# Narrowing weights on dense buffers, w_out's forms in w_in's ring, both score halves in one PSUM bank

## The chip, the cores and the metric

The kernel runs on one core of a Trainium2 chip. The metric is the device time of one execution in microseconds (us); the time shown is the median of the runs. The profile comes from one execution, and its times are counted from the first instruction of the program.

The engines are called by short names. PE is TensorE, which multiplies matrices, and PEld is its loading of weights, which overlaps the multiplying. DVE is VectorE, ACT is ScalarE, POOL is GpSimd, and SP is SyncE, which here does nothing but issue DMAs. L12 is line 12 of the kernel before.

## What is computed

Channel attention on q, k, v (4 batches, 6080 tokens, 256 channels), then a feed-forward layer with Gelu:

```python
qn = q / (norm(q, axis=1) + 1e-06);  kn = k / (norm(k, axis=1) + 1e-06)
s = kn.transpose(0, 2, 1) @ qn / tau          # 256 x 256 for each batch
a = softmax(s, axis=-1)                       # denominator + 1e-09
x = (v @ a).reshape(24320, 256)
h = x @ w_in                                  # 256 -> 2048
out = gelu(h) @ w_out                         # 2048 -> 256
```

q, k and v are float32. w_in and w_out reach the kernel as 64-bit floats, two 32-bit words to a value, and are narrowed on the chip.

## The kernel before

**Arithmetic.** A float32 operand is split into a high part in the matmul's own type (fp32r) and a low part that holds the rest. A product is then three matmuls: high by low, high by high, low by high. The softmax's matrix is multiplied into w_in for each batch (`w_group`, `w_product`), so v goes straight into the feed-forward layer. Most products of blocks are made by a scheme with seven products in place of eight. It needs sums of blocks, the forms: `v_sums` for v, `w_adds` for w_in, `wo_adds` for w_out. `wo_forms`, `wo_adds`, `wo_hi` and `wo_lo` (L586 to L615) make the forms S1 to S4 of w_out from its plain blocks, four times, once for each group g, and store them to DRAM (`keep_out`), from where all later steps load them again.

**Prelude.** The scores of batch 0 are plain float32 matmuls (`qk_first`, L431) while q and k stream in. `qk_fill` begins batch 1's scores: 16 float32 matmuls, each of them two instructions in the profile (L443), which are put between the stages of the first softmax. `GAPS` says how many go before the stages' matmuls, and what is left over runs after `w_group(0, 0)`.

**Narrowing.** There are 16 units of weights, 512 values a partition each: two units for each of four groups of w_in and eight for w_out. `load_unit` loads one as pairs of 32-bit words into a ring `raw` of three buffers (or, for two of them, into `raw_w`), and `narrow_unit` calls `narrow` (L520 to L549). Of a pair, word 1 is `high` and word 0 is `low`; both are views with a step of two words. `narrow` clamps `high`, squares it on ACT, shifts and merges its bits, masks by the square, scales `low` by the exponent, and leaves high and low parts of the float32 value. Of its ten steps, eight are on DVE (L532, L537, L539, L541, L544, L545, L548, L549) and two on ACT (L534, L547). Clamped and merged values are written back into `high`, in the strided buffer. Scratch is `nt` in the prelude, and then by turns the buffers `kqc` and `osb` of the main part. Narrowed units are stored to DRAM too (`keep`, L1107); stores that come early are held and issued after the loads of q and k.

Five units are narrowed in the prelude and eleven in the part that follows, `paces` of them after each step u. Units 0 to 3 are w_in's groups 0 and 1; unit 4 is the first of w_out, and `pair_out` multiplies by it during u = 1.

**Plain part.** Eight steps u make the first 1024 tokens with ordinary block products (`plain_products`, L847 to L849). `pair_out` (L981 to L983) multiplies Gelu's blocks of the step before by w_out, interleaved with them.

**Main part.** After that come steps of one chunk and one group each, with seven products (`chunk_ops`, L903 to L905), Gelu (L930, L933), the splitting of its result (L936, L954) and the products with w_out (`chunk_out`). Four more kinds of work are hung on these steps by number: the sums of v, the forms of w_out (step g + 1 of the first four), the next batch's scores, and its softmax with its w_groups.

**Next batch's scores.** `burst(b, k, m)` multiplies four splits of k and q for one half m of the channels: for each, one matmul of 512 columns (high k by high and low q) and one of 256 (low k by high q). It writes to the bank that this step has spare. `burst_sum` adds the bank to `sacc` in SBUF, once for each half. There are 34 pairs of bursts. Softmax adds `sacc`'s two halves (high and low) at its start (L636).

**What sets the order.** The prelude keeps the order in which it is written and its priorities. From `w_group(0, 0)` on, a planner (`Order`) takes all instructions of PE, ACT, DVE and SP, keeps PE's order as written, gives each other instruction a latest start from PE's nominal times, and runs a list schedule with modelled durations 24 times, each time earlier for what PE waited on; the best order is fixed for each engine. Buffers in rings (`RINGS`: raw 3, hl 2, wo 4, win 2) must be taken in turn. The model's durations count elements and know nothing of steps between them. Each engine runs its own order strictly, so an instruction that waits holds up all behind it; SP's DMAs are one such queue.

Of the kernel before, what the change touches and what calls it, by code (L numbers as in the profile page):

```python
# [9 lines left out]
F32 = mybir.dt.float32  # L10
# [307 lines left out]
GAPS = (7, 4, 2)  # L318
# [17 lines left out]
def channel_attention_gelu_ffn(ctx, tc, qk, kqt, vt, tau, w_in, w_out, out):  # L336
# [100 lines left out]
    def qk_fill():  # L437
# [9 lines left out]
        acc = state["sacc"] = pm.tile([P, NCT, NT], F32, name="sacc")  # L447
        nc.gpsimd.memset(acc[:, :, C:], 0.0)
        for m in range(NCT):
            nc.vector.tensor_copy(out=acc[:, m, 0:C].rearrange("p (b a) -> p b a", a=2), in_=paired(s[:, m]))  # L450
# [19 lines left out]
    def burst(b, k, m):  # L470
        cs = slice(m * P, (m + 1) * P)
        s = state["burst"] = spare()
        ops = [(hls[b, k * NB + t], j) for t in range(NB) for j in range(JS)]
        for i, (hl, j) in enumerate(ops):
            nc.tensor.matmul(s, hl[:, 0, j, 0, cs], hl[:, :, j, 1].rearrange("p h (a b) -> p h b a", a=2), start=(i == 0), stop=False,
                             skip_group_check=True)
            nc.tensor.matmul(s[:, 0:C], hl[:, 1, j, 0, cs], paired(hl[:, 0, j, 1]), start=False,
                             stop=(i == len(ops) - 1), skip_group_check=True)

    def burst_sum(k, m):  # L480
        s = state.pop("burst")
        if k == 0:
            if m == 0:
                state["sacc"] = pm.tile([P, NCT, NT], F32, name="sacc")
            nc.vector.tensor_copy(out=state["sacc"][:, m], in_=s)
        else:
            acc = state["sacc"][:, m]
# [21 lines left out]
    def load_w(src):  # L509

        if len(units) in (11, 12):
# [6 lines left out]
    def narrow(hi, lo, raw):  # L518
# [4 lines left out]

        if "filled" not in state:
            tmp = pst.tile([P, 2, n], F32, name="nt", bufs=2)
        else:
            state["nt"] = not state.get("nt")
            tmp = pg.tile([P, 2, n], F32, name="kqc" if state["nt"] else "osb", bufs=1)

        top = high.bitcast(F32)  # L530
# [12 lines left out]
        body = high  # L543
# [42 lines left out]
    def wo_forms(g):  # L586
        whole = pg.tile([P, 8 * H], F32, name="osb")
        x = whole.rearrange("p (s f q n) -> p s f q n", s=2, f=4, q=2)
        hl = whole[:, 0:4 * H].rearrange("p (f h q n) -> p f h q n", f=2, h=2, q=2).bitcast(F32R)
        return x, [pg.tile([P, 2, 2, 2, P], F32R, name="kqc", bufs=1), hl]  # L590
# [15 lines left out]
    def wo_hi(x, hl):  # L606
        for i in range(2):
            nc.scalar.copy(out=hl[i][:, :, 0], in_=x[:, 1, 2 * i:2 * i + 2])

    def wo_lo(g, x, hl):  # L610
        for i in range(2):
            nc.vector.tensor_tensor(out=hl[i][:, :, 1], in0=x[:, 1, 2 * i:2 * i + 2], in1=f32(hl[i][:, :, 0]),
                                    op=ALU.subtract)
# [878 lines left out]
```

## Time and profile before

| | |
|---|---|
| median of 3 runs | 2061.69 us (2061.46 to 2065.83) |
| the profiled execution | 2062.65 us, span of its instructions 2060.9 us |
| granted PE clock, mean | 0.997 |
| busy: PE, PEld, DVE, ACT | 99%, 95%, 90%, 79% of the span |
| chain of work that ended last | PE 87%, DVE 6%, DMA 3%, ACT 2%, issue 1% |

A row of a group gives line, engine and operation, then output and inputs by the program's names, the shapes, how often, the busy time and the mean duration. A row of the waits gives the engine and line that waited, what ended the wait, the total in us, how often, and the longest. A row of a timeline gives start, duration and instruction, and in brackets how long the engine was idle before it and what ended that. A row of a stretch gives its ends, its length, busy time and instruction count of PE, PEld, DVE, ACT and POOL, the granted PE clock (1.00 is full), the DMA engines' share and GB/s. Matmuls are pipelined: a busy time of a single one is longer than the distance to the next, which is what counts.

### The profile page before, as it was taken

The numbers are of one execution on the slowest core, as the hardware profiler recorded it, in microseconds if no ns is written. First come the engines' busy times: TensorE is split into PE (matmuls) and PEld (weight loads), VectorE is DVE, ScalarE is ACT, GpSimd is POOL, SyncE is SP. The second block draws the span as 40 slices with busy tenths as digits, with TensorE's granted clock in tenths as the row PEclk, the third lists the DMA queues.
The fourth block names the chain that finished last, engine by engine and source line by source line (L and its number), as shares of the span: only waits on it lengthen the run. The fifth ranks groups of instructions, "written<-read, shape, count | busy, mean of one in ns | idle before, by whom it ended". The sixth has DMA issues, their size and how long they took to land.

```text
span 2060.9 us, 40753 instructions
## 1 busy us (share of the span) xinstructions
PE 2032.2 (99%) x15958; PEld 1962.3 (95%) x15958; DVE 1857.9 (90%) x2733; ACT 1620.7 (79%) x2720; POOL 1.3 (0%) x8
## 2 busy tenths in 40 slices
PE   8899999999999999999999999999999999999999
PEld 7778999999999999999999999999999999999999
DVE  6899899899899989999989999999998998898897
ACT  6666788888888888888988877777787777777776
POOL 0000000000000000000000000000000000000000
PEclk9999999999999999999999999999999999999999
DMA  9556687877787778687678666666556566566664
GB/s 376 177 187 220 225 277 239 270 262 258 245 298 253 244 252 273 223 279 257 225 267 267 206 225 225 215 211 213 198 185 224 177 200 214 189 202 206 199 196 166
DMA packets 153808, 475.31 MB, mean 231 GB/s; under 512 B 16016, under 2 KB 26256, under 8 KB 153104
## 3 DMA queue, kind: packets, MB, share of 16 engines
q1 hardware_dynamic: 153616, 472.71, 68.3%
q8 instruction: 125, 2.05, 0.4%
q14 instruction: 67, 0.55, 0.1%
HBM read 435.16 MB, written 37.49 MB: 229 GB/s over the span
## 4 chain that ended last, share of the span: by engine, by line
PE 87%; DVE 6%; DMA 3%; ACT 2%; issue 1%; SPq 0%; DVEq 0%; ACTq 0%
PE po L1038 10%; PE po L1037 10%; PE po L1036 10%; PE pb L903 5%; PE pb L904 5%; PE pb L905 5%; PE pa L903 5%; PE pa L904 5%; PE pa L905 5%; PE po L1020 4%; PE po L1022 4%; PE po L1021 4%; DMA raw<-qk 2%; PE pz L904 2%; PE pz L905 2%; PE pz L903 2%
## 5 line engine op out<-in xcount | busy, mean ns | idle before, releaser
L1038 PE MATMUL po<-los,wo 128*128 128x256 f32 (+1 forms) x1890 | 520.3, 275 | 0.8 <-DVE los L954 0.8
L1036 PE MATMUL po<-his,wo 128*128 128x256 f32 (+1 forms) x1890 | 520.4, 275 | 0.0
L1037 PE MATMUL po<-his,wo 128*128 128x256 f32 (+1 forms) x1890 | 519.9, 275 | 0.0
L936 DVE TENSOR_TENSOR los<-gs,his 128x512 fp32r<-128x512 f32 (+1 forms) x601 | 407.0, 682 | 67.9 <-ACT gs L930 53.4
L1036 PEld LDWEIGHTS po<-his,wo 128*128 128x128 f32 x1890 | 362.7, 192 | 1.9
L1038 PEld LDWEIGHTS po<-los,wo 128*128 128x128 f32 x1890 | 362.9, 192 | 1.3 <-DVE los L954 1.2
L1037 PEld LDWEIGHTS po<-his,wo 128*128 128x128 f32 x1890 | 362.9, 192 | 0.5
L954 DVE TENSOR_TENSOR los<-gs,his 128x1024 fp32r<-128x1024 f32 (+1 forms) x270 | 326.6, 1210 | 18.2 <-ACT his L950 16.6
L950 ACT CAST his<-gs 128x1024 fp32r<-128x1024 f32 (+1 forms) x270 | 281.2, 1043 | 75.3 <-DVE gs L947 73.2
L903 PE MATMUL pa<-vhi,wl 128*128 128x256 f32 (+1 forms) x920 | 253.3, 275 | 4.7 <-DVE pz L917 4.4
L903 PE MATMUL pb<-vhi,wl 128*128 128x256 f32 (+1 forms) x920 | 253.6, 276 | 3.1 <-ACT gs L930 1.3
L904 PE MATMUL pa<-vhi,wh 128*128 128x256 f32 (+1 forms) x920 | 253.2, 275 | 0.0
L905 PE MATMUL pa<-vlo,wh 128*128 128x256 f32 (+1 forms) x920 | 253.2, 275 | 0.0
L905 PE MATMUL pb<-vlo,wh 128*128 128x256 f32 (+1 forms) x920 | 253.1, 275 | 0.0
L904 PE MATMUL pb<-vhi,wh 128*128 128x256 f32 (+1 forms) x920 | 253.1, 275 | 0.0
L943 DVE TENSOR_TENSOR gs<-gs 128x1024 f32<-128x1024 f32 (+1 forms) x135 | 163.7, 1213 | 29.8 <-ACT gs L930 26.2
L903 PEld LDWEIGHTS pa<-vhi,wl 128*128 128x128 f32 x920 | 176.2, 191 | 9.9 <-DVE pz L917 5.8
L903 PEld LDWEIGHTS pb<-vhi,wl 128*128 128x128 f32 x920 | 176.3, 192 | 6.9 <-ACT his L933 1.5
L933 ACT ACTIVATE his<-px 128x512 fp32r<-128x512 f32 (+1 forms) x184 | 108.8, 591 | 90.7 <-PE px L905 88.6
L904 PEld LDWEIGHTS pa<-vhi,wh 128*128 128x128 f32 x920 | 176.3, 192 | 3.6
L904 PEld LDWEIGHTS pb<-vhi,wh 128*128 128x128 f32 x920 | 176.3, 192 | 2.4
L905 PEld LDWEIGHTS pa<-vlo,wh 128*128 128x128 f32 x920 | 176.8, 192 | 0.0
(284 smaller groups left out, 5138.7 us busy)
## 6 DMA issues: line engine op xcount, KB each, us to landing
wo<-keep_out SPq DMA_DIRECT2D x503, 512.0 KB, 4.5
raw<-qk SPq DMA_DIRECT2D x95, 512.0 KB, 6.1
kqc<-kqt SPq DMA_DIRECT2D x72, 512.0 KB, 5.1
wo<-keep_out SPq DMA_DIRECT2D x135, 256.0 KB, 4.0
v_raw<-vt SPq DMA_DIRECT2D x40, 512.0 KB, 6.6
out<-osb SPq DMA_DIRECT2D x40, 512.0 KB, 5.1
win<-keep_in SPq DMA_DIRECT2D x24, 512.0 KB, 6.1
keep_in<-win SPq DMA_DIRECT2D x4, 1024.0 KB, 4.4
```

Of the source, the lines that this page charges most:

```text
L903: nc.tensor.matmul(o, wls[g][:, a, q], paired(vh[:, at, :h]), start=start, stop=False, skip_group_check=True)
L904: nc.tensor.matmul(o, whs[g][:, a, q], paired(vh[:, at, :h]), start=False, stop=False, skip_group_check=True)
L905: nc.tensor.matmul(o, whs[g][:, a, q], paired(vl[:, at, :h]), start=False, stop=stop, skip_group_check=True)
L933: nc.scalar.activation(out=slot(name)[0], in_=t[SOURCE[name]], func=AF.Gelu)
L936: tt(out=slot(name)[1], in0=whole(name), in1=f32(slot(name)[0]), op=ALU.subtract)
L943: tt(out=g4[:, 0:2], in0=g4[:, 1:3], in1=g4[:, 0:2], op=ALU.subtract)
L950: nc.scalar.copy(out=views[1][:, 2 - 2 * i:4 - 2 * i], in_=views[0][:, 2 * i:2 * i + 2])
L954: tt(out=views[2][:, at], in0=views[0][:, 2 * i:2 * i + 2], in1=f32(views[1][:, at]), op=ALU.subtract)
L1020: nc.tensor.matmul(o, w[:, 1, q], mh, start=start, stop=False, skip_group_check=True)
L1036: nc.tensor.matmul(o, w[:, 1, q], mh, start=starts and q == 0, stop=False, skip_group_check=True)
L1037: nc.tensor.matmul(o, w[:, 0, q], mh, start=False, stop=False, skip_group_check=True)
L1038: nc.tensor.matmul(o, w[:, 0, q], ml, start=False, stop=stops and q == 1, skip_group_check=True)
```

## The change

1. *Narrowing.* Once the main buffers are open, `narrow` puts the clamped value, the merged bits and the mask into a dense buffer (`p5`, or a third part of `osb`), in place of word 1 of the raw pairs.
2. *w_out's first unit.* The prelude narrows four units in place of five; the fifth, and the stores that were held, come after `w_group(0, 0)`, in the planned part. Its raw words go to the ring `raw`.
3. *Fills.* `GAPS` is 10, 4, 2, so that all 16 float32 matmuls of batch 1 stand among the stages of the first softmax and none after `w_group(0, 0)`.
4. *Forms of w_out.* Their high and low parts lie in one buffer of the ring `win` in place of `kqc` and half of `osb`; one cast and one subtraction of 1024 values replace two of 512. The two stores stay.
5. *Scores.* The two halves m share one PSUM bank, 256 columns each. The matmul of 512 columns becomes two of 256, all three products are added up in PSUM, one addition to `sacc` replaces two, `sacc` has half the size, and softmax takes its values from there without adding halves.

```diff
@@ -315,7 +315,7 @@
 
 NARROWS = (4, 9)
 
-GAPS = (7, 4, 2)
+GAPS = (10, 4, 2)
 
 TOP_MAX = (2.0 - 2.0 ** -3 - 2.0 ** -23) * 2.0 ** 16
 TOP_MIN = 1.125 * 2.0 ** -15
@@ -444,10 +444,9 @@
                     s[:, m], raw[:, j, 0, m * P:(m + 1) * P], raw[:, j, 1], start=(i == 0 and m == 0),
                     stop=(i == FILL * JS - 1), skip_group_check=True)
                 yield
-        acc = state["sacc"] = pm.tile([P, NCT, NT], F32, name="sacc")
-        nc.gpsimd.memset(acc[:, :, C:], 0.0)
+        acc = state["sacc"] = pm.tile([P, NCT, C], F32, name="sacc")
         for m in range(NCT):
-            nc.vector.tensor_copy(out=acc[:, m, 0:C].rearrange("p (b a) -> p b a", a=2), in_=paired(s[:, m]))
+            nc.vector.tensor_copy(out=acc[:, m].rearrange("p (b a) -> p b a", a=2), in_=paired(s[:, m]))
 
 
     def sum_up(nps, acc, start, stop):
@@ -469,22 +468,21 @@
 
     def burst(b, k, m):
         cs = slice(m * P, (m + 1) * P)
-        s = state["burst"] = spare()
-        ops = [(hls[b, k * NB + t], j) for t in range(NB) for j in range(JS)]
-        for i, (hl, j) in enumerate(ops):
-            nc.tensor.matmul(s, hl[:, 0, j, 0, cs], hl[:, :, j, 1].rearrange("p h (a b) -> p h b a", a=2), start=(i == 0), stop=False,
-                             skip_group_check=True)
-            nc.tensor.matmul(s[:, 0:C], hl[:, 1, j, 0, cs], paired(hl[:, 0, j, 1]), start=False,
+        if m == 0:
+            state["burst"] = spare().rearrange("p (m c) -> p m c", m=NCT)
+        s = state["burst"][:, m]
+        ops = [(hls[b, k * NB + t], j, x) for t in range(NB) for j in range(JS) for x in ((1, 0), (0, 0), (0, 1))]
+        for i, (hl, j, (x, y)) in enumerate(ops):
+            nc.tensor.matmul(s, hl[:, x, j, 0, cs], paired(hl[:, y, j, 1]), start=(i == 0 and m == 0),
                              stop=(i == len(ops) - 1), skip_group_check=True)
 
-    def burst_sum(k, m):
+    def burst_sum(k):
         s = state.pop("burst")
         if k == 0:
-            if m == 0:
-                state["sacc"] = pm.tile([P, NCT, NT], F32, name="sacc")
-            nc.vector.tensor_copy(out=state["sacc"][:, m], in_=s)
+            state["sacc"] = pm.tile([P, NCT, C], F32, name="sacc")
+            nc.vector.tensor_copy(out=state["sacc"], in_=s)
         else:
-            acc = state["sacc"][:, m]
+            acc = state["sacc"]
             nc.vector.tensor_tensor(out=acc, in0=s, in1=acc, op=ALU.add)
 
     norms = {}
@@ -508,7 +506,7 @@
 
     def load_w(src):
 
-        if len(units) in (11, 12):
+        if len(units) == 12:
             raw = pst.tile([P, src.shape[-1], 2], U32, name="raw_w", bufs=2)
         else:
             raw = pqk.tile([P, src.shape[-1], 2], U32, name="raw", bufs=3)
@@ -521,13 +519,18 @@
         n = raw.shape[1]
         low, high = raw[:, :, 0], raw[:, :, 1]
 
+        own = None
         if "filled" not in state:
             tmp = pst.tile([P, 2, n], F32, name="nt", bufs=2)
         else:
             state["nt"] = not state.get("nt")
-            tmp = pg.tile([P, 2, n], F32, name="kqc" if state["nt"] else "osb", bufs=1)
-
-        top = high.bitcast(F32)
+            if state["nt"]:
+                tmp, own = pg.tile([P, 2, n], F32, name="kqc", bufs=1), pg.tile([P, NT], F32, name="p5")
+            else:
+                tmp = pg.tile([P, 3, n], F32, name="osb", bufs=1)
+                own = tmp[:, 2]
+
+        top = high.bitcast(F32) if own is None else own
         body, w, tail = tmp[:, 0].bitcast(U32), tmp[:, 0], tmp[:, 1]
         nc.vector.tensor_scalar(out=top, in0=high.bitcast(F32), scalar1=TOP_MAX, scalar2=-TOP_MAX,
                                 op0=ALU.min, op1=ALU.max)
@@ -540,7 +543,7 @@
                                        op0=ALU.bitwise_and, op1=ALU.bitwise_or)
         nc.vector.scalar_tensor_tensor(out=w, in0=tail, scalar=TOP_MIN ** 2, in1=top, op0=ALU.is_ge, op1=ALU.mult)
 
-        body = high
+        body = topu
         nc.vector.tensor_scalar(out=body, in0=w.bitcast(U32), scalar1=0xFF800000, scalar2=None, op0=ALU.bitwise_and)
         nc.vector.scalar_tensor_tensor(out=tail, in0=low, scalar=2.0 ** -52, in1=body.bitcast(F32), op0=ALU.mult,
                                        op1=ALU.mult)
@@ -586,8 +589,8 @@
     def wo_forms(g):
         whole = pg.tile([P, 8 * H], F32, name="osb")
         x = whole.rearrange("p (s f q n) -> p s f q n", s=2, f=4, q=2)
-        hl = whole[:, 0:4 * H].rearrange("p (f h q n) -> p f h q n", f=2, h=2, q=2).bitcast(F32R)
-        return x, [pg.tile([P, 2, 2, 2, P], F32R, name="kqc", bufs=1), hl]
+        t = pw.tile([P, 2, NCT, NT], F32R, name="win", bufs=2)
+        return x, t.rearrange("p a b n -> p (a b n)").rearrange("p (f h q n) -> p f h q n", f=4, h=2, q=2)
 
     def wo_adds(g, x):
         fa, fs = x[:, 0], x[:, 1]
@@ -604,15 +607,12 @@
         tt(out=s4, in0=a12, in1=s2, op=ALU.subtract)
 
     def wo_hi(x, hl):
-        for i in range(2):
-            nc.scalar.copy(out=hl[i][:, :, 0], in_=x[:, 1, 2 * i:2 * i + 2])
+        nc.scalar.copy(out=hl[:, :, 0], in_=x[:, 1])
 
     def wo_lo(g, x, hl):
-        for i in range(2):
-            nc.vector.tensor_tensor(out=hl[i][:, :, 1], in0=x[:, 1, 2 * i:2 * i + 2], in1=f32(hl[i][:, :, 0]),
-                                    op=ALU.subtract)
-        nc.sync.dma_start(out=keep_out[g][:, 0:4:3], in_=f32(hl[0]))
-        nc.sync.dma_start(out=keep_out[g][:, 4:6], in_=f32(hl[1]))
+        nc.vector.tensor_tensor(out=hl[:, :, 1], in0=x[:, 1], in1=f32(hl[:, :, 0]), op=ALU.subtract)
+        nc.sync.dma_start(out=keep_out[g][:, 0:4:3], in_=f32(hl[:, 0:2]))
+        nc.sync.dma_start(out=keep_out[g][:, 4:6], in_=f32(hl[:, 2:4]))
 
 
     def preload(func, after):
@@ -627,14 +627,11 @@
         rk, nms, dens = (small[:, 16 + 2 * i:18 + 2 * i] for i in range(3))
         ts = []
         for m in range(NCT):
-            t = pm.tile([P, C], F32, name=f"t{m}")
             if first:
+                t = pm.tile([P, C], F32, name=f"t{m}")
                 nc.scalar.copy(out=t, in_=state["s"][m])
             else:
-                s = state["sacc"]
-                both = s[:, m].rearrange("p (h b a) -> p h a b", h=2, a=2)
-                nc.vector.tensor_tensor(out=t.rearrange("p (a b) -> p a b", a=2), in0=both[:, 0], in1=both[:, 1],
-                                        op=ALU.add)
+                t = state["sacc"][:, m]
             ts.append(t)
         nsum = state.pop("nsum")
         if first:
@@ -669,8 +666,12 @@
         if not first:
             yield
         for m in range(NCT):
-            nc.vector.scalar_tensor_tensor(out=ts[m], in0=ts[m], scalar=rk[:, m:m + 1], in1=rq[:, 0:C],
-                                           op0=ALU.mult, op1=ALU.mult)
+            t, x, o = ts[m], rq[:, 0:C], ts[m]
+            if not first:
+                o = ts[m] = pm.tile([P, C], F32, name=f"t{m}")
+                t = t.rearrange("p (b a) -> p a b", a=2)
+                x, o = (y.rearrange("p (a b) -> p a b", a=2) for y in (x, o))
+            nc.vector.scalar_tensor_tensor(out=o, in0=t, scalar=rk[:, m:m + 1], in1=x, op0=ALU.mult, op1=ALU.mult)
             nc.vector.reduce_max(out=nms[:, m:m + 1], in_=ts[m], axis=AX.X, negate=True)
         yield
         es = []
@@ -1154,10 +1155,8 @@
             narrow_unit()
         if 14 <= js < 18:
             v_split_first((B11, B21, B12, B22)[js - 14])
-    for _ in range(3):
+    for _ in range(2):
         narrow_unit()
-    for x in held:
-        keep(*x)
     fill = qk_fill()
     stages = softmax(True, ps_o, "po2")
     with tc.high_priority():
@@ -1186,6 +1185,9 @@
     body = nc.cur_bb.bb.instructions
     opened = len(body)
     w_group(0, 0)
+    narrow_unit()
+    for x in held:
+        keep(*x)
     for _ in fill:
         pass
     for _ in range(3):
@@ -1243,7 +1245,8 @@
             w = (4 if b == 1 else 3) + 3 * k
             for m in range(NCT):
                 put(n0 + w, "PE", burst, b, k, m)
-                put(n0 + w, "PEdve", burst_sum, k, m)
+            put(n0 + w, "PEdve", lambda: None)
+            put(n0 + w, "PEdve", burst_sum, k)
             for i in range(NB):
                 js = k * NB + i
                 put(max(0, n0 + w - 4 + i), "load", load_qk, b, js)
```

## The prediction

> **What bounds the kernel now.** I read the busy times by stretch first, to find where TensorE (PE) is not full.
>
> ```profile
> 80.00:160.00 80.00, 76.92 (x344) 65.46 (x343) 79.06 (x133) 53.59 (x92) 0.00 (x0) 0.98 0.56 175
> ...
> 240.00:500.00 260.00, 260.00 (x2136) 254.48 (x2136) 237.36 (x329) 219.39 (x369) 0.00 (x0) 1.00 0.78 264
> 500.00:530.00 30.00, 28.28 (x221) 26.73 (x220) 26.81 (x54) 29.24 (x50) 0.00 (x0) 1.00 0.66 222
> ```
>
> The columns are PE, weight loads, VectorE (DVE), ScalarE (ACT), GpSimd, clock, DMA share, GB/s. From 240 us on PE has no gap (260.00 of 260), so there every extra matmul costs its full time, and work taken from DVE buys nothing. From 80 to 160 us it is DVE that is full (79.06 of 80) and PE that has holes. So the change can win only ahead of 240 us and can lose behind it. Who waits for whom between 60 and 240 us:
>
> ```profile
> PE pa L847 <- DVE wl L721: 4.2, 1, 4.2
> ...
> DVE raw L532 <- DMA raw<-w_out: 3.6, 1, 3.6
> PE pa L903 <- DVE pz L917: 3.4, 2, 3.0
> ...
> DVE osb L598 <- DMA keep_out<-osb: 1.3, 1, 1.3
> ```
>
> Each PE hole has a tail, which the clock column of narrower stretches shows:
>
> ```profile
> 69.58:75.21 5.63, 5.63 (x12) 4.03 (x13) 1.85 (x5) 2.48 (x6) 0.00 (x0) 0.50 0.82 234
> ...
> 129.80:132.92 3.12, 3.12 (x9) 2.46 (x8) 3.05 (x7) 1.71 (x3) 0.00 (x0) 0.51 1.04 402
> 219.09:221.90 2.81, 2.81 (x11) 2.54 (x11) 2.70 (x6) 1.16 (x3) 0.00 (x0) 0.50 0.73 265
> 100.00:115.00 15.00, 14.69 (x69) 12.55 (x68) 14.85 (x26) 10.52 (x18) 0.00 (x0) 1.00 0.61 207
> 115.00:126.00 11.00, 10.40 (x48) 8.57 (x47) 10.90 (x19) 4.93 (x9) 0.00 (x0) 1.00 0.66 192
> 126.00:134.00 8.00, 5.83 (x20) 4.46 (x19) 7.93 (x14) 4.52 (x8) 0.00 (x0) 0.79 0.66 221
> ```
>
> Behind the 4.2 us hole PE runs 5.63 us at half clock and loses 2.8; behind the hole at 126 us 3.12 us (1.6 lost); behind the 3.0 us hole at 215 us 2.81 us (1.4 lost). [...]
>
> **The change, part by part.** *w_out's first unit in the scheduled part, and the loads behind it.* Now its steps sit in the prelude, and ACT runs its cast ahead of the first weight scaling:
>
> ```profile
> 66.71 0.62 ACT L547 CAST wo<-nt 128x512 fp32r<-128x512 f32 x1 [2.87 <-DVE nt L541]
> 67.24 0.68 ACT L733 ACTIVATE hl<-pb,rden 128x512 f32<-128x512 f32 x1
> ```
>
> L733 feeds L720 and L721, for which PE waits 4.2 us. The cast had ACT idle for 2.87 us, and L721 is behind the unit's last steps on DVE too. In the changed kernel the planner places this unit after w_group's matmuls, where pair_out needs it only in the second u, so I take nearly the whole 4.2 us as gone at that place. What counts over the stretch is DVE's queue, since DVE is full until 160 us: the unit's DVE work isn't less, but it falls into the 3.6 us in which DVE stood before L532 waiting for `raw<-w_out`. Those loads stood on SP behind the four keep_out stores of the same unit; now units 5 and 6 have free slots of the ring and needn't wait for these stores. Gain 3.6 us; bounds 0 (the hole opens again behind another store) and 3.6. The two keep_in stores and the four keep_out stores are the same DMAs, later on SP; their only readers come after 100 us.
>
> *Narrowing on dense buffers.* The strided steps of a unit in the scheduled part:
>
> ```profile
> L537 DVE TENSOR_SCALAR kqc<-raw x6: 496/553/570, 76.0 to 153.4; 128x512 uint32<-128x512 uint32 x6
> L534 ACT ACTIVATE kqc<-raw x6: 875/932/1008, 80.6 to 148.0; 128x512 f32<-128x512 f32 x6
> L539 DVE SCALAR_TENSOR_TENSOR raw<-raw,kqc x6: 857/898/908, 81.6 to 154.5; 128x512 uint32<-128x512 uint32 x6
> L541 DVE SCALAR_TENSOR_TENSOR kqc<-kqc,raw x6: 829/834/856, 82.5 to 155.4; 128x512 f32<-128x512 f32 x6
> L544 DVE TENSOR_SCALAR raw<-kqc x6: 460/514/560, 84.6 to 156.3; 128x512 uint32<-128x512 uint32 x6
> L545 DVE SCALAR_TENSOR_TENSOR kqc<-raw x6: 748/842/860, 86.2 to 157.3; 128x512 f32<-128x512 uint32 x6
> ...
> L549 DVE TENSOR_TENSOR wo<-kqc x4: 674/691/693, 87.6 to 160.2; 128x512 fp32r<-128x512 f32 x4
> ```
>
> L549 of the same units, all dense, takes 691 ns in the same stretch, while L539 and L541, the same size and two operands as well, take 898 and 834. Ahead of 55 us the same lines took:
>
> ```profile
> L537 DVE TENSOR_SCALAR nt<-raw x3: 427/427/427, 10.6 to 50.3; 128x512 uint32<-128x512 uint32 x3
> L539 DVE SCALAR_TENSOR_TENSOR raw<-raw,nt x3: 683/684/702, 11.3 to 53.0; 128x512 uint32<-128x512 uint32 x3
> L541 DVE SCALAR_TENSOR_TENSOR nt<-nt,raw x3: 683/691/693, 12.1 to 53.7; 128x512 f32<-128x512 f32 x3
> L544 DVE TENSOR_SCALAR raw<-nt x3: 420/421/431, 13.8 to 54.5; 128x512 uint32<-128x512 uint32 x3
> ```
>
> I take these as the dense price, since they are the nearest rows: 898 - 684 = 0.21, 834 - 691 = 0.14, 553 - 427 = 0.13, 514 - 421 = 0.09 us, and 0.07 for L545, which keeps one strided operand (half of 842 - 691). That is 0.64 us of DVE a unit, 7.0 us over 11 units. Bounds: 0 (dense is no faster) and 0.84 a unit, 9.2 us (L532, still strided on one side, and all of L545 gain as well). Nothing excludes a small loss, but L549's row makes one unlikely. Square (L534) gets off ACT's 0.93 us too, at no gain: ACT is busy 53.59 of 80.
>
> DVE's end of that stretch comes 3.6 + 7.0 earlier. A less loaded DVE also waits more for the others: it idled 0.9 of 80 us when full, and I take as much again off. Front: 3.6 + 7.0 - 0.9 = 9.7 us. PE can take it: its holes there are 4.2 + 0.3 + 0.6 + 2.2 and its half-clock losses 2.8 + 1.6, together 11.7.
>
> *Three fills ahead of the first softmax matmul.* They are the six instructions that now run under the 4.2 us hole:
>
> ```profile
> 56.69 0.70 PE L668 MATMUL po<-diag,ones 128*128 128x256 f32 x2 [0.86 <-DVE diag L663]
> ...
> 63.95 1.46 PE L443 MATMUL po<-raw 128*128 128x256 f32 x6
> ```
>
> They go into the 0.86 us before L668 and may overhang by 1.46 - 0.86 = 0.6; the first softmax chain waits for that. The overhang counts full cycles with their pipeline tail, so I take 0.2 us of loss (0 to 0.6).
>
> *w_out's forms in the ring of w_in.* L598 of the next unit no longer waits for keep_out to leave osb: 1.3 us of DVE, in order ahead of L917, for which PE waits 3.0 us at 215 us. The hole should shrink to 1.7, and with it the half-clock tail of 1.4 should go. I take 2.5 of these 2.7. Bounds: 0 (another wait holds L917) and 4.4 (hole and tail). Two casts and two subtractions become one each at the same element count. The ring's loads for the second batch, which the planner could start early, now queue behind the forms; their first matmuls are at step 37, so they have time.
>
> *One bank for both halves.* A burst's matmuls change shape:
>
> ```profile
> 626.25 0.38 PE L475 MATMUL pa<-hl 128*128 128x512 f32 x1
> ...
> 627.23 0.28 PE L1036 MATMUL po<-his,wo 128*128 128x256 f32 x1
> ...
> 628.90 0.28 PE L1036 MATMUL po<-his,wo 128*128 128x256 f32 x1
> ```
>
> Three pairs of 512 and 256 columns take 627.23 - 626.25 = 0.98 us, 0.327 each. From 627.23 to 628.90 stand 15 matmuls of 256 columns, 0.111 each, so three of them are 0.334. There are 34 bursts x 2 x 4 = 272 pairs: 272 x 0.007 = 2.0 us of loss, on a full PE. Bounds 1.0 and 3.0. DVE's adds halve, under cover of PE. One wait falls away, of the second half's matmuls on the first half's copy:
>
> ```profile
>   PEld pa L475: 0.3, 1
> ```
>
> I add 0.5 us for the holes of 500 to 530 us, where two L636 adds vanish from a DVE queue that is busy 26.81 of 30; bounds 0 and 1.7, all of PE's idle time there.
>
> **Sum.** 9.7 + 2.5 + 0.3 + 0.5 - 0.2 - 2.0 = 10.8 us. The profiled execution took 2062.65 us, 0.96 above the median of 2061.69. 2062.65 - 10.8 = 2051.85, on the scale of the median 2050.9, say 2051.
>
> **The rivals.** (1) *Dense buffers buy nothing.* The slow rows could come from where the tiles lie and not from the stride. Against it: L549 is fast in the same tiles and stretch. Without the 7.0 us the gain is 3.8: 2058. [...]
>
> (2) *DMA keeps the times.* The loads stay behind stores on SP (3.6 back) and the forms' place is held by another transfer (2.5 back): 10.8 - 6.1 = 4.7, 2057. For it: L598's and L532's waits both end with a DMA.
>
> (3) *All of PE's holes go:* 11.7 in the front, 4.4 at the forms, 1.7 + 0.3 later, less 2.2: 15.9, 2046. For it: nothing else holds PE there; against: DVE stays 99% busy.
>
> (4) *Slower: the one bank makes a wait.* The single add now comes only after both halves, and the next step's first product takes the same bank, so L903 may wait for it. It turns the sum at 10.8 / 34 = 0.32 us a burst; at 0.5 us it costs 17, giving 2050.9 + 17 = 2068. Against: the last add of a burst stands at the same place today, and the only wait on record for sacc's instructions is the 0.3 above.
>
> **How the numbers follow.** Forecast 0.57 (own range 2047 to 2056), rival 1 0.10, rival 2 0.15, rival 3 0.12, rival 4 0.06. The range 2042 to 2060 reaches to rivals 1 and 3 with 2 to 4 us for the planner's new order, and leaves out rival 4 and tails. 0.2% is 4.1 us, about what can be told from no change: faster means below 2057.6. Faster: 0.57 + 0.12 + 0.10 of rival 2 + 0.02 of rival 1 = 0.81; slower 0.06; same 0.13.
>
> **What would show it.** Right: L847's first wait below 1.5 us and no half clock behind it; no wait of L532 on `raw<-w_out` near 72 us; L539 and L541 near 690 ns; no L598 wait on keep_out; the three burst lines at 0.111 us each. Wrong: L539 still near 900 ns, PE holes of more than 2 us between 70 and 230 us, or L903 waiting for sacc's add.

## The result, and the profile after

| | before | after |
|---|---|---|
| median | 2063.76 us (2061.46 to 2067.07) | 2048.19 us (2047.71 to 2049.54) |
| ratio, 95% interval | | 0.9924 (0.9907 to 0.9942) |
| span of the profiled execution | 2060.9 us | 2045.9 us |
| chain that ended last | PE 87%, DVE 6%, DMA 3% | PE 93%, DVE 4%, DMA 0% |

The change gains 15.6 us, where 10.8 were forecast. The time before is here the median of four runs, the three from above and one more of 2067.07 us; against their median of 2061.69 the gain is 13.5, and the two profiled executions differ by 15.0. Lines behind L447 have moved by up to three in the new kernel, up or down: L535 is the old L532, L542 the old L539, L848 the old L847. Each kernel of the experiments has line numbers of its own, too. The busy times by stretch of the kernel after (length, PE, weight loads, DVE, ACT, POOL, clock, DMA share, GB/s):

```profile
80.00:160.00 80.00, 78.06 (x363) 66.89 (x362) 78.28 (x137) 54.32 (x96) 0.00 (x0) 1.00 0.56 177
180.00:220.00 40.00, 40.00 (x300) 38.30 (x299) 37.83 (x65) 32.37 (x56) 0.00 (x0) 1.00 0.85 293
240.00:500.00 260.00, 259.43 (x2163) 254.28 (x2162) 236.06 (x339) 220.33 (x373) 0.00 (x0) 1.00 0.77 261
500.00:530.00 30.00, 29.60 (x257) 28.89 (x255) 27.28 (x44) 27.67 (x48) 0.00 (x0) 1.00 0.82 265
```

and of the kernel before, for 180 to 220 us:

```profile
180.00:220.00 40.00, 35.26 (x228) 32.17 (x228) 35.22 (x70) 25.83 (x46) 0.00 (x0) 0.98 0.67 220
```

DVE is still nearly full from 80 to 160 us (78.28 of 80), and PE still has holes there. The clearest difference is 180 to 220 us: 35.26 us of PE before, 40.00 after. From 240 to 500 us PE now has small holes where it had none, and from 500 to 530 fewer than before (29.60 us busy, from 28.28).

The steps of the narrowing in the kernel after (min, median and max in ns, first and last start in us; the own dense buffer is called `p` in the profile; these are the six units with scratch in `kqc`, and those with scratch in `osb` have medians within 20 ns of them):

```profile
L535 DVE TENSOR_SCALAR p<-raw x6: 486/492/525, 63.2 to 129.2; 128x512 f32<-128x512 f32 x6
L537 ACT ACTIVATE kqc<-p x6: 629/631/661, 63.8 to 134.0; 128x512 f32<-128x512 f32 x6
L540 DVE TENSOR_SCALAR kqc<-p x6: 396/418/426, 63.8 to 138.5; 128x512 uint32<-128x512 uint32 x6
L542 DVE SCALAR_TENSOR_TENSOR p<-p,kqc x6: 674/691/691, 64.5 to 138.9; 128x512 uint32<-128x512 uint32 x6
L544 DVE SCALAR_TENSOR_TENSOR kqc<-kqc,p x6: 673/692/734, 65.2 to 139.6; 128x512 f32<-128x512 f32 x6
L547 DVE TENSOR_SCALAR p<-kqc x6: 408/423/470, 66.5 to 140.8; 128x512 uint32<-128x512 uint32 x6
L548 DVE SCALAR_TENSOR_TENSOR kqc<-raw,p x6: 683/838/844, 67.5 to 141.3; 128x512 f32<-128x512 uint32 x6
```

L542, L544, L540 and L547 have the dense price that was forecast (684, 691, 427 and 421 ns, from 898, 834, 553 and 514). L548, which still reads word 0 with a step, did not move: 842 before, 838 now.

The first wait of PE did not go as forecast. Its row among the waits, and the stretch behind it:

```profile
PE pa L848 <- DVE wl L722: 2.6, 1, 2.6
```

```profile
66.30:70.00 3.70, 3.70 (x9) 2.65 (x10) 2.81 (x7) 2.30 (x6) 0.00 (x0) 0.59 0.92 293
```

2.6 us are left of the 4.2, and a tail at half clock follows (0.59 over 3.70 us, 0.51 from 67.30 to 70.40). The timelines of ACT and DVE in that place (start, duration, instruction, idle time before it):

```profile
62.25 0.21 ACT L621 ACTIVATE junk<-eh 128x2 f32<-128x2 f32 x1
63.81 0.63 ACT L537 ACTIVATE kqc<-p 128x512 f32<-128x512 f32 x1 [1.36 <-issue]
64.35 0.67 ACT L734 ACTIVATE hl<-pb,rden 128x512 f32<-128x512 f32 x1
```

```profile
63.24 0.49 DVE L535 TENSOR_SCALAR p<-raw 128x512 f32<-128x512 f32 x1
63.76 0.43 DVE L540 TENSOR_SCALAR kqc<-p 128x512 uint32<-128x512 uint32 x1
64.11 0.42 DVE L449 COPY sacc<-po 128x256 f32<-128x256 f32 x1
64.47 0.69 DVE L542 SCALAR_TENSOR_TENSOR p<-p,kqc 128x512 uint32<-128x512 uint32 x1
65.20 0.69 DVE L544 SCALAR_TENSOR_TENSOR kqc<-kqc,p 128x512 f32<-128x512 f32 x1
65.81 0.42 DVE L722 TENSOR_TENSOR wl<-hl,wh 128x256 fp32r<-128x256 f32 x1
```

The planner put the moved unit's steps ahead of the weight scaling on both engines: its Square (L537) stands ahead of L734 on ACT and has ACT idle for 1.36 us, and four of its DVE steps stand ahead of L722, for which PE waits.

To compare kernels I use one sum throughout: PE's holes, for each matmul of the trace the distance to the next start less the distance that its shape takes undisturbed (in the kernel before 0.216 us for 512 columns, ten of them from 123.69 to 125.85 us, and 0.111 for 256, from 627.23 to 628.90), so that half-clock tails count too. It is worked out from the profiled execution of each kernel; what the last row has beyond the others lies ahead of 50 us and behind 840. In us:

| stretch | before | after | dense alone | forms alone | dense + forms |
|---|---|---|---|---|---|
| 50 to 82 | 9.6 | 6.1 | 9.8 | 9.9 | 9.3 |
| 82 to 165 | 6.0 | 3.2 | 1.8 | 5.9 | 2.5 |
| 165 to 240 | 7.7 | 0.1 | 7.8 | 0.7 | 0.0 |
| 240 to 495 | 0.1 | 1.3 | 0.1 | 1.8 | 2.5 |
| 495 to 540 | 3.3 | 1.5 | 3.5 | 1.5 | 1.5 |
| 540 to 840 | 3.1 | 0.6 | 3.6 | 2.2 | 2.2 |
| whole span | 39.8 | 22.9 | 36.5 | 31.0 | 26.0 |

16.9 us of holes are gone, and the span is 15.0 shorter: 1.9 us went into more PE work.

### The profile page after: what moved, and what is told of

Same layout as the page of the kernel before. It is cut to its first block, busy times and chain, and to the rows that moved or that the text cites. A ratio compares the mean times of both kernels' runs of the same rounds, so it can differ in the third digit from the quotient of the medians.

```text
span 2045.9 us, 41248 instructions
## 1 busy us (share of the span) xinstructions
PE 2029.7 (99%) x16230; PEld 1970.5 (96%) x16230; DVE 1833.1 (90%) x2689; ACT 1610.8 (79%) x2714; POOL 0.8 (0%) x7
## 4 chain that ended last, share of the span: by engine, by line
PE 93%; DVE 4%; ACT 2%; issue 1%; DMA 0%; SPq 0%; DVEq 0%; ACTq 0%
PE po L1039 10%; PE po L1038 10%; PE po L1037 10%; PE pb L904 5%; PE pb L905 5%; PE pb L906 5%; PE pa L904 5%; PE pa L905 5%; PE pa L906 5%; PE po L1021 4%; PE po L1023 4%; PE po L1022 4%; PE pb L476 2%; PE pa L476 2%; PE pz L905 2%; PE pz L906 2%
## 5 line engine op out<-in xcount | busy, mean ns | idle before, releaser
L955 DVE TENSOR_TENSOR los<-gs,his 128x1024 fp32r<-128x1024 f32 (+1 forms) x270 | 326.6, 1210 | 23.3 <-ACT his L951 22.2
L906 PEld LDWEIGHTS pb<-vlo,wh 128*128 128x128 f32 x920 | 176.6, 192 | 0.0
```

The source lines that it names most:

```text
L906: nc.tensor.matmul(o, whs[g][:, a, q], paired(vl[:, at, :h]), start=False, stop=stop, skip_group_check=True)
L955: tt(out=views[2][:, at], in0=views[0][:, 2 * i:2 * i + 2], in1=f32(views[1][:, at]), op=ALU.subtract)
```

## The experiments

Each part was undone in the changed kernel, three sets of parts were made alone in the kernel before, the planner's view of its start was changed, and two probes, which leave the whole computation out, measured strided steps on DVE. Times are medians, ratios are to the kernel before on the same chip, with the 95% interval.

**1. Narrowing undone** (clamped values and masks go back into the strided words):

```diff
-            if state["nt"]:
-                tmp, own = pg.tile([P, 2, n], F32, name="kqc", bufs=1), pg.tile([P, NT], F32, name="p5")
-            else:
-                tmp = pg.tile([P, 3, n], F32, name="osb", bufs=1)
-                own = tmp[:, 2]
+            tmp = pg.tile([P, 2, n], F32, name="kqc" if state["nt"] else "osb", bufs=1)
...
-        body = topu
+        body = high
```

> The changed kernel, with narrowing back on the strided words (its steps write into word 1 of the raw pairs again). Theory A (strided steps are slow by 0.64 us a unit and DVE bounds the plain part): 12 units x 0.64 = 7.7 us of DVE come back, of which PE's present slack in the plain part hides some; 4 to 8 us slower than the changed kernel, 2052 to 2056, with L539-like steps near 0.90 us and PE holes of over 1 us again between 80 and 165 us. Rival (dense buffers buy nothing; the place of the tiles did it): within 1.5 us of the changed kernel, 2047 to 2050.

Measured: 2055.02 us, ratio 0.9967 (0.9954 to 0.9979), 6.8 us above the changed kernel. The same steps on strided words, and the stretch from 80 to 160 us:

```profile
L537 DVE SCALAR_TENSOR_TENSOR raw<-raw,kqc x6: 694/888/941, 64.2 to 146.5; 128x512 uint32<-128x512 uint32 x6
L539 DVE SCALAR_TENSOR_TENSOR kqc<-kqc,raw x6: 693/842/876, 64.9 to 147.5; 128x512 f32<-128x512 f32 x6
```

```profile
80.00:160.00 80.00, 73.55 (x324) 62.23 (x324) 76.47 (x126) 50.87 (x88) 0.00 (x0) 0.96 0.48 150
```

The steps are slow again (888 and 842 ns against 691 and 692), and 80 to 160 us has 73.55 us of PE in place of 78.06. So dense buffers are worth something, and rival 1's time falls. The edit puts back the step of two words and the tile `raw` together, so by itself it does not tell them apart. Against the tile speaks that the same steps took 684 and 691 ns in `raw` ahead of 55 us; runs 11 and 12 take the question up.

**2. The unit moved back**, with the held stores and its raw words in `raw_w`:

```diff
-        if len(units) == 12:
+        if len(units) in (11, 12):
...
-    for _ in range(2):
+    for _ in range(3):
         narrow_unit()
+    for x in held:
+        keep(*x)
...
     w_group(0, 0)
-    narrow_unit()
-    for x in held:
-        keep(*x)
```

> The changed kernel, with w_out's first unit narrowed in the prelude again. Theory A: PE's wait before its first plain product goes from 2.6 back to about 4.2 us, DVE's 3.6 us hole before the first unit's loads comes back; 3 to 6 us slower than the changed kernel, 2051 to 2054. Rival (DVE isn't the bound any more once the buffers are dense, so the hole is covered): 0.5 to 2 us slower, only the first wait's difference, 2049 to 2050.

Measured: 2048.68 us, ratio 0.9932 (0.9919 to 0.9944). No difference to the changed kernel that can be told. Yet the waits of 50 to 90 us are back:

```profile
PE pa L848 <- DVE wl L722: 4.7, 1, 4.7
DVE p L535 <- DMA raw<-w_out: 3.8, 1, 3.8
```

The holes of 50 to 82 us grow by 3.0 us (9.1), those of 82 to 165 us shrink by 1.1 (2.1). The DMA wait is real, and the move takes it away, but it gives almost nothing to the end: 0.5 us by the medians, 1.4 between the profiled executions. The rival, that the hole is covered once the buffers are dense, comes nearest. But in run 1, with strided steps and the unit moved, the holes of 50 to 165 us come to 16 us, as many as in the kernel before (15.6), so there the move gave nothing either. The unit alone in the kernel before was not run.

**3. Forms undone** (high and low parts in `kqc` and half of `osb` again, two casts and two subtractions):

```diff
-        t = pw.tile([P, 2, NCT, NT], F32R, name="win", bufs=2)
-        return x, t.rearrange("p a b n -> p (a b n)").rearrange("p (f h q n) -> p f h q n", f=4, h=2, q=2)
+        hl = whole[:, 0:4 * H].rearrange("p (f h q n) -> p f h q n", f=2, h=2, q=2).bitcast(F32R)
+        return x, [pg.tile([P, 2, 2, 2, P], F32R, name="kqc", bufs=1), hl]
...
```

> The changed kernel, with w_out's forms in kqc and half of osb again. The changed kernel has lost all of PE's 7.7 us of holes between 165 and 240 us, where 2.5 were forecast. Theory A (osb was the cause of all of them: each group's sums wait for the stores of the group before): 5 to 8 us slower than the changed kernel, 2053 to 2056, with the wait on keep_out back. Rival (the ring is worth the forecast 2.5 and the rest went because PE and DVE reach that place in better order): 1 to 3 us slower, 2049 to 2051.

Measured: 2053.56 us, ratio 0.9954 (0.994 to 0.9968), 5.4 us lost. Its waits from 82 to 245 us (L601, L907 and L921 here are the old L598, L903 and L917) and its stretch of 180 to 220 us:

```profile
PE pb L907 <- DVE pz L921: 1.9, 1, 1.9
...
DVE osb L601 <- DMA keep_out<-osb: 1.3, 1, 1.3
```

```profile
180.00:220.00 40.00, 38.07 (x267) 35.78 (x267) 33.73 (x62) 26.38 (x47) 0.00 (x0) 0.96 0.70 230
```

The wait on the store of `osb`, 1.3 us as before, is back, and with it PE's wait on L921; the holes of 165 to 240 us are 4.8, from 0.1. That is what theory A had.

**4. Two banks again** (the old burst, two sums, softmax adds the halves):

```diff
-        if m == 0:
-            state["burst"] = spare().rearrange("p (m c) -> p m c", m=NCT)
-        s = state["burst"][:, m]
+        s = state["burst"] = spare()
...
```

> The changed kernel, with a PSUM bank for each half of the scores and 512-column matmuls again. Theory A (272 x 7 ns more of PE in a stretch where PE is full, DVE's relief hidden): undoing it makes the changed kernel 1 to 2.5 us faster, 2045.7 to 2047.2. Rival (the halved adds and the missing wait for the first half's copy take away PE holes between 165 us and the end that cost more than the matmuls): undoing it makes it 1 to 5 us slower, 2049 to 2053.

Measured: 2047.8 us, ratio 0.9928 (0.9916 to 0.9941): the same as the changed kernel, with the same span of 2045.9 us. Its PE holes are 24.8 us, 1.9 more than the changed kernel's 22.9. So one bank does cost its matmuls 1.8 to 1.9 us of PE, as the step said (2.0), and the holes differ by as much the other way. From 240 to 840 us they are 5.6 us with two banks and 3.4 with one; why those close, by fewer adds on DVE or by another order of the planner, isn't shown. From 50 to 82 us it is two banks that have less, 4.5 against 6.1: behind the same first wait of PE, 2.6 us, the granted clock stayed full there (1.00 over 55 to 82 us, 0.94 in the changed kernel), where the changed kernel ran at half (0.51 from 67.30 to 70.40). So the equal spans rest in part on the clock of one execution.

**5. Dense narrowing alone** in the kernel before:

> The kernel before, with the dense buffers of narrowing alone. Taken out of the changed kernel they cost 6.8 us. Theory A (DVE's 0.64 us a unit is worth the same alone): 5 to 9 us faster than before, 2054 to 2058. Rival (it needs the moved unit, which fills DVE's 3.6 us hole, to be worth much): 1 to 4 us faster, 2059 to 2062.

Measured: 2057.65 us, ratio 0.9972 (0.9961 to 0.9983), a gain of 5.5 us.

**6. Forms alone** in the kernel before:

> The kernel before with the forms in the ring of w_in alone. Theory A (own price, whatever DVE does): 2063 - 5.4 = 2058, the holes of 165 to 240 us gone from 7.7 to below 2. Theory B (DVE, still late with strided words, puts off the same matmuls, so the hole moves and stays): 2061 to 2063, holes of more than 5 us in all between 82 and 240 us beyond what they lose.

Measured: 2054.26 us, ratio 0.9959 (0.9947 to 0.9972), a gain of 8.8 us, more than either theory had. The holes of 165 to 240 us are 0.7, below the 2 of theory A.

**7. Dense narrowing and forms**, without unit, fills and bank:

> The kernel before with two of the five parts, dense narrowing and the forms in the ring of w_in; unit, fills and burst stay as before. Theory A (these two parts are the whole gain; the other three come to nothing, as their undoing did): 2047 to 2050 us, the holes of 165 to 240 us at most 1 us instead of the 7.8 that dense narrowing alone left. Theory B (each part has its own price and no more: 5.5 us for dense narrowing alone and 5.4 for the forms, as lost when undone): 2063 - 10.9 = 2052. Theory C (the forms gain only behind the moved unit): about 2057, with the holes of 165 to 240 us still there.

Measured: 2049.11 us, ratio 0.9934 (0.992 to 0.9947), a gain of 14.0 us. Its holes fall by 13.8 us, and so does its span: these parts add no work on PE. Here are 180 to 220 us for the three, first dense alone:

```profile
180.00:220.00 40.00, 35.64 (x216) 32.43 (x216) 33.98 (x65) 25.17 (x45) 0.00 (x0) 0.91 0.68 224
```

then the forms alone:

```profile
180.00:220.00 40.00, 40.00 (x275) 37.55 (x274) 36.62 (x67) 32.48 (x57) 0.00 (x0) 1.00 0.80 271
```

and both:

```profile
180.00:220.00 40.00, 40.00 (x280) 37.71 (x279) 37.49 (x66) 32.58 (x56) 0.00 (x0) 1.00 0.84 286
```

The forms close this stretch (35.26 to 40.00) with DVE's strided steps as slow as ever, and dense narrowing does next to nothing for it (35.64); its own place is 82 to 165 us (6.0 to 1.8 in the table). The two parts have different stretches, so their gains add up (5.5 + 8.8 = 14.3, measured 14.0), and together they are the change but for 0.9 us of time (1.6 of gain), which the runs can't tell from nothing. PE's first wait and DVE's wait on the load both stand in this kernel as in the one before (L849, L723 and L537 are the old L847, L721 and L532):

```profile
PE pa L849 <- DVE wl L723: 4.2, 1, 4.2
...
DVE p L537 <- DMA raw<-w_out: 3.5, 1, 3.5
```

**8. Seven fills ahead of the first softmax matmul**, as before the change:

```diff
-GAPS = (10, 4, 2)
+GAPS = (7, 4, 2)
```

> The changed kernel with seven fills ahead of the first softmax matmul instead of ten. My step gave the three fills a loss of 0.2 us (0 to 0.6) in the chain of the first softmax. Theory A (that step): 2048.0, no difference that can be told, and a PE hole of 0.7 to 0.9 us before the first softmax matmul. Theory B (without the three fills, they run later between 56 and 66 us, where PE now waits 2.6 us, and fill that hole): 2046 to 2047. Theory C (the planner orders all work behind them anew): more than 2050.

Measured: 2049.47 us, ratio 0.9934 (0.9922 to 0.9947), 1.3 above the changed kernel, less than the runs can tell for certain; the two profiled executions differ by 2.9. The timelines of PE and DVE show what the fills do:

```profile
56.11 0.70 PE L665 MATMUL po<-diag,ones 128*128 128x256 f32 x2 [0.84 <-DVE diag L660]
...
63.40 1.46 PE L443 MATMUL po<-raw 128*128 128x256 f32 x6
67.88 0.80 PE L848 MATMUL pa<-vhi,wl 128*128 128x512 f32 x1 [3.02 <-DVE wl L722]
```

```profile
63.77 0.69 DVE L552 TENSOR_TENSOR win<-nt 128x512 fp32r<-128x512 f32 x1
64.89 0.43 DVE L535 TENSOR_SCALAR p<-raw 128x512 f32<-128x512 f32 x1 [0.43 <-PE po L443]
```

and DVE's L552 in the changed kernel:

```profile
62.46 0.69 DVE L552 TENSOR_TENSOR win<-nt 128x512 fp32r<-128x512 f32 x1
```

With seven, the 0.84 us hole ahead of L665 is there, as theory A had it, and six fill instructions run from 63.40 us on; they do not fill PE's wait, as theory B had it, which is 3.02 us. The first product starts at 67.88 us, in the changed kernel at 66.28. Only a part of these 1.6 us is a wait for the fills: DVE waits 0.43 us for them. It is 1.3 us late before that, at L552, the last step of the fourth unit (63.77, from 62.46). That unit's first step runs at 58.30 us behind the softmax's L674 here, and at 56.42 ahead of it in the changed kernel. So at this place the three fills are no loss of 0.2; they win 1.6 us, most of it by another order on DVE.

**9. The planner's view of its start.** It takes ACT and DVE as free when it begins; the trace has DVE busy for some 2.7 us more and ACT for 2.0. Told so, it should not put the moved unit ahead of the weight scaling:

```diff
-        free, order, slip, dma, events = [0.0] * 4, [], 0.0, 0.0, [0.0]
+        free, order, slip, dma, events = [0.0, 2000.0, 2700.0, 0.0], [], 0.0, 0.0, [0.0, 2000.0, 2700.0]
```

> The changed kernel, and the planner is told that ACT is busy for the first 2.0 us and DVE for the first 2.7 us of its part (in the changed kernel's trace PE starts that part at 60.47 us, ACT comes free of the prelude at 62.46 and DVE at 63.15). In the changed kernel ACT runs the moved unit's Square (L537) ahead of the first weight scaling (L734) and waits 1.36 us for DVE, and PE then waits 2.6 us for L722. Theory C (the planner's order of the moved unit is what's left of that wait): PE's wait falls under 1.5 us and the half-clock tail behind it goes; 1 to 4 us faster than the changed kernel, 2044.2 to 2047.2. Rival (DVE bounds the plain part, so the time comes back as holes between 82 and 165 us): within 1 us of the changed kernel, 2047.2 to 2049.2.

Measured: 2052.61 us, ratio 0.9952 (0.994 to 0.9965), 4.4 slower than the changed kernel. The first two stretches:

```profile
55.00:82.00 27.00, 25.66 (x117) 20.95 (x116) 24.87 (x57) 20.44 (x41) 0.00 (x0) 1.00 0.56 199
82.00:165.00 83.00, 76.53 (x359) 65.02 (x358) 80.43 (x141) 53.91 (x95) 0.00 (x0) 1.00 0.55 173
```

The first wait nearly goes (holes of 50 to 82 us from 6.1 to 2.6, full clock), and the next stretch loses more than that: its holes go from 3.2 to 8.3. The rival named that place but had no loss. So this order, the only other one tried, wins nothing by closing the hole.

**10. The same with two banks:**

> The same start times for the planner, with a bank for each half of the scores and 512-column matmuls as in the kernel before. With two banks the changed kernel had the same span (2045.9 us) with 1.8 us more of PE holes. Theory C: the holes of 82 to 165 us (4.5 us with two banks) shrink with the better start, and the 2 us less of matmuls show: 2042.5 to 2046.5. Rival (the order is drawn anew with every edit, and the 2 us are lost in it): 2046 to 2049.

Measured: 2050.61 us, ratio 0.9943 (0.993 to 0.9955). The same picture, and slower than both forecasts: 2.7 us of holes from 50 to 82 us, 8.4 from 82 to 165.

**11. Strided steps by themselves.** A program of two DVE steps of 128x512 on every second word and on dense words:

> A small kernel that measures the disputed cost by itself and leaves all of the reference's computation out: DVE runs ten two-operand steps and five one-operand steps of 128x512 float32, on every second word or on dense words, with PE idle, with PE streaming fp32r matmuls of 256 columns, with PE streaming plain float32 matmuls, and with ACT copying 128x1024 values. Theory A1 (strided words are slow only beside another reader of SBUF, and fp32r matmuls are that reader): two-operand steps 0.68 us dense in all cases, and strided 0.68 to 0.70 with PE idle or on float32, 0.85 to 0.90 beside fp32r. Rival A2 (ACT is the reader): strided 0.68 beside fp32r and 0.85 to 0.90 beside ACT's copies. Rival A3 (not the stride but the place of the tiles): strided and dense alike in every case.

Measured, with fp32r matmuls of 256 dense columns beside them, strided and then dense:

```profile
L56 DVE SCALAR_TENSOR_TENSOR rsr<-rsr,body x10: 629/687/691, 22.3 to 33.0; 128x512 f32<-128x512 f32 x10
```

```profile
L56 DVE SCALAR_TENSOR_TENSOR rdr<-rdr,body x10: 679/684/690, 25.4 to 36.4; 128x512 f32<-128x512 f32 x10
```

Both are alike here, and likewise with PE idle, with float32 matmuls and with copies on ACT (all medians 677 to 696 ns). The step alone isn't slow, and neither partner of theories A1 and A2 makes it so.

**12. Strided steps beside what PE really reads.** All matmuls of the plain and main part take their moving columns in pairs (`paired`, "p (a b) -> p b a"), the scores and fills of the prelude do not. This probe adds that:

> Leaves out all of the reference's computation: one two-operand and one one-operand step of 128x512 float32 on DVE, on every second word and on dense words, beside PE with (1) fp32r, 512 dense columns, (2) fp32r, 256 columns taken in pairs, as the bursts take them, (3) 512 columns in pairs with dense copies on ACT, (4) 256 columns in pairs with copies on ACT and loads on the DMA queue. Theory A (one of these partners makes strided words slow): from that phase on the strided steps take 0.85 to 0.90 and 0.51 to 0.55 us, the dense ones 0.68 and 0.42. Theory B (none of them does): all phases near 0.68 and 0.42 for both, and the cause in the main part stays open.

Measured on DVE (`rs` is strided, `rd` dense; they alternate), with PE on 512 dense columns:

```profile
L64 DVE SCALAR_TENSOR_TENSOR rs<-rs,body 128x512 f32<-128x512 f32 x16 | 10.9, 683 | 0.0
L64 DVE SCALAR_TENSOR_TENSOR rd<-rd,body 128x512 f32<-128x512 f32 x12 | 8.2, 686 | 0.0
```

with PE on 256 columns in pairs, ACT and DMA idle:

```profile
L64 DVE SCALAR_TENSOR_TENSOR rd<-rd,body 128x512 f32<-128x512 f32 x6 | 4.1, 690 | 0.0
L64 DVE SCALAR_TENSOR_TENSOR rs<-rs,body 128x512 f32<-128x512 f32 x4 | 3.0, 748 | 0.0
```

and with 512 columns in pairs, copies on ACT and loads:

```profile
L64 DVE SCALAR_TENSOR_TENSOR rs<-rs,body 128x512 f32<-128x512 f32 x7 | 6.0, 853 | 0.0
L64 DVE SCALAR_TENSOR_TENSOR rd<-rd,body 128x512 f32<-128x512 f32 x5 | 3.5, 695 | 0.0
```

Theory A holds in the main, on a few steps in each stretch: the strided step took 683 ns beside 512 dense columns and 748 beside 256 columns in pairs (the neighbouring dense steps 690), and 853 beside 512 columns in pairs with copies on ACT and loads, near the 898 of the kernel before. That 256 dense columns left it at 687 in run 11 leaves the pairs as the partner, not the number of columns. How much each of the others adds isn't told apart: 256 columns in pairs with copies on ACT gave 807 against 724. In one stretch, 512 columns in pairs with ACT mostly idle, dense steps took up to 900 ns too (817 on average, strided 892), so dense words are not proof against it.

## Why the prediction was right, and where it wasn't

*Dense narrowing, 7.0 us: right.* Undone it costs 6.8, alone it brings 5.5. The row prices were right for four of the five steps. The fifth, "0.07 for L545, which keeps one strided operand", was 0: one strided operand kept the whole price here (838 against 842). The prediction's own row of L541 says so, which has one strided operand and 834 ns. The argument that L549 is fast in the same tiles was the right one, and the prelude's rows were the right bound.

*w_out's first unit, 3.6 us, and "nearly the whole 4.2 us as gone at that place": wrong.* 0.5 us by the undoing. The failed step is "the planner places this unit after w_group's matmuls". It put the steps ahead of the weight scaling, which keeps 2.6 us of the wait. And the 3.6 us that DVE wins before the load do not come out at the end: with the unit moved back the holes of 50 to 82 us grow by 3.0, of which 1.1 come back by 165 us. The planner's order of all that follows is another in each kernel, which moves holes of 1 to 2 us about. The reading of the DMA wait itself was right: in the changed kernel no wait of L535 (the old L532) on `raw<-w_out` is left there.

*Forms, 2.5 us: mechanism right, term too small.* 5.4 undone, 8.8 alone. The sum took one hole of 3.0 us and its tail of 1.4, 4.4 as the bound. The stretch of 180 to 220 us had PE at 35.26 of 40 in a row that the prediction did not read; with tails the holes of 165 to 240 us were 7.7, and the forms alone take 7.0 of them away. A second wait of the kernel before, at 187.7 us, is part of that, and it hung on DVE as well:

```profile
PE po L1022 <- DVE los L936: 1.7, 1, 1.7
```

Ahead of that L936 DVE ran the forms' adds and the first subtraction nearly without a break, from 182.58 to 186.40 us. With the forms in the ring their steps lie spread among the others, and this wait is gone in both kernels of runs 6 and 7. How much of it is the free buffer and how much the new order, isn't told apart. This is the term of the sum that was sized worst: 2.5 against 5 to 9.

*Fills, -0.2: sign wrong.* The overhang was 0.12 us (L729 begins at 60.47, at 60.35 with seven), as forecast. What the sum left out is that the place of the fills changes DVE's order in the prelude too: 1.6 us at the first product, of which DVE's wait for the fills is 0.43. At the end it is 1.3 us, which the runs can't tell from nothing. In the kernel before the fills did lie hidden under the 4.2 us hole: DVE worked without a break from 60.34 us up to L721 at 69.11.

*One bank, -2.0: right as PE work (1.8 to 1.9), not seen as time.* "From 240 us on PE has no gap (260.00 of 260), so there every extra matmul costs its full time" was read from a row that ends at 500 us; from 240 to 840 us the kernel before has 6.5 us of holes, the changed kernel 3.4, and 5.6 with two banks. Undoing the bank moves the end by nothing that can be told. Rival 4 did not come: no wait of PE on the sum is among the waits.

*Holes of 500 to 530, 0.5: 1.8 came (3.3 to 1.5), and not by the two adds.* Forms alone give 1.5 with the adds in place; the kernel without the forms, but with one bank, has 1.4; with the forms and two banks (run 4) it is 2.3. So neither part alone explains them. Holes of 2.5 us in all around 825 us, which the prediction did not see, are gone there in every kernel but the one with dense narrowing alone; runs 3, 6 and 7 have one of 1.2 to 1.3 us at 769 to 803 us instead.

*The whole.* Put by place, the sum was near everywhere: between 50 and 240 us 12.0 forecast (9.7 + 2.5 - 0.2) and 13.9 of holes gone (23.3 to 9.4); ahead of 50 us nothing and 0.8; behind 240 us 0.8 (0.3 + 0.5) and 2.2 (10.6 to 8.4); PE's work -2.0 and -1.9. That is 10.8 against 15.0 us of span. Put by part it was wrong: the unit got 3.6 us of which 0.5 came, and the forms, with 2.5, brought 5 to 9. That the time still fell into the range is partly luck, since these errors have opposite signs. Rival 3's time of 2046 lay nearer than 2051, but not by its way, since 9.4 us of holes are left between 50 and 240 us. Rival 2 fell in both halves: neither the wait on `raw<-w_out` nor that on `keep_out<-osb` is among the waits.

## What to carry to other kernels

Price an operand's step from the row of the same instruction beside the same neighbours, not from a stage in which the other engines read otherwise (one and the same L539: 684 and 898 ns). Where one engine is late, sum PE's holes by stretch with their tails before pricing a cause, since the one wait that the list names can be half of what hangs on it (at the forms 4.4 us with its tail, of 7.7). A hole just ahead of a stage in which another engine is full was worth little here (0.5 us by the medians of run 2): the two parts that worked were those that took work or waits from DVE where it was late, and the one that moved work past the hole gave next to nothing.

## What the runs showed of the hardware that was not expected

A two-operand DVE step on every second 4-byte word of a 128x512 float32 tile was as fast as on dense words beside 512 dense columns on PE (683 and 686 ns); beside moving columns in pairs it took 748 to 853 ns where dense steps took 690 to 724, and in one stretch 892 beside 817. It fits the 684 ns of the strided L539 in the prelude and its 898 behind it; the kernel itself was not run with PE on dense columns there. What makes the step slow there, these runs don't show.

The granted clock fell to half behind some PE holes of 2 to 3 us and not behind others, so the prediction's "Each PE hole has a tail" is too wide. In the kernel before it was 0.51 from 129.80 to 132.92 us behind a hole of 2.17 us, and 0.50 from 219.09 to 221.90 behind one of 3.0. Behind a hole of 2.6 us at PE's first plain product the changed kernel had 0.51 from 67.30 to 70.40 us, and the kernel of run 4, behind a hole as long at the same product, had 1.00 over the whole of 55 to 82 us. Where it fell behind these holes, it stayed so for 2.81 to 3.12 us, and the hole cost about 1.5 us more than its length (3.12 x 0.49); behind the hole of 4.2 us it was 5.63 us, and 2.8 were lost. What decides it, these traces don't show; as an estimate from these rows, 1.5 us of difference between two single executions can come from it alone.
